# Attention and max-of-three feed-forward on one core: scaled float16 pairs with resident weights, exponentials in place in PSUM, weighted sums as one column-tiled step

## The chip, the cores and the metric

The kernel runs on one core of one Trainium2 chip. The metric is device time in microseconds (us). Before the change the median of three runs is 1806.76 us (1802.73 to 1811.37).

## What is computed

Eight batches, twelve heads, 448 tokens, 64 numbers per head. Queries and keys are divided by their root mean square over the 64 numbers and multiplied by a gain each; softmax attention follows; the heads of a batch are put side by side to a 3584x768 matrix x, and a feed-forward layer takes the elementwise maximum of three products:

```
q_n, k_n = rmsnorm(q, g_q), rmsnorm(k, g_k)
scores = q_n @ k_n.T / sqrt(64);  attn = softmax(scores)
x = (attn @ v), heads side by side                  # 3584 x 768
h = max(x @ w1, x @ w2, x @ w3)                      # 3584 x 768
out = h @ w_out
```

The four weights come as float64, everything else and the output are float32: the kernel reads a weight as pairs of 32-bit words and puts the float32 together with bit operations ("decode").

## The kernel before, in words

**Groups.** The work is cut into 48 groups g (six pairs of heads in each of eight batches). Per group the two heads' queries and keys are loaded in rows (load_q, load_kv, L167 to L193), squared and summed (squares L196, inv_rms L207, its power on POOL at L218), scaled (scale_q L221, scale_k L239), split into two float16 parts, high and low (part_rows L256), and turned to columns by a DMA transpose (turn_rows L267). A product of two numbers in two parts takes three matmuls (TERMS L317: high by high, high by low, low by high).

**Softmax.** The 448 queries of a group are four chunks c of 112. scores (L319) writes a chunk into a PSUM tile sc of two banks, one per head; the pool ps_s has two such tiles. scores is called for chunks 0 and 1 together and later for 2 and 3 together. softmax (L338) takes the row maximum on DVE (L340), a product (nm, L342) and two exponentials on ACT (L348) that write a float32 tile p in SBUF; after them sc is free. weights (L355) takes the reciprocal of the sums (rs, L359 and L362), the scaled high part on ACT (L365) and the low part on DVE (L366), which reads p and the high part pp from SBUF. turn_weights (L372) turns pp with a DMA transpose issued by SP (L377).

**Weighted sums.** add_values (L383) is called once per step with one block u of keys: the stationary operand is a block of v in both parts, 128 columns wide (64 high, 64 low), the moving one a part of the weights; the high and low columns come out in two halves of the partitions, in one PSUM tile per head (av, pool ps_a of two). fold (L403) adds the halves with one ACT and one DVE instruction per head (L409, L410), and finish (L415) splits x into a high part on ACT and a low part on POOL (L418, L419), both in fp32r (a float32 form that TensorE takes in one pass). The scale of v is found per group by a matmul with ones into a corner of sc (bound_v L288, L290) and three small DVE instructions, L292 to L297; PE and SP have their order written by hand, and the scores of the second two chunks stand behind that corner.

**Feed-forward.** ffn (L515) is a generator. layer1 (L449) does, per block ft of 128 outputs and per j of the three weights, 18 matmuls of 448 columns (L458) in six pieces of three; layer2 (L494) does per 128 tokens and half of the outputs 18 matmuls of 384 columns (L502). Before a layer1 unit, fetch (L428) loads its 384 KB of float32 weights from a scratch array in DRAM, and split_w (L437) makes high and low parts: an ACT cast (L112) and a POOL subtraction (L113). This is done anew for every batch, 144 times. The units' results are maxed on DVE (L472) and split on ACT and POOL (L477, L478).

**Decode.** prep_w (L147) loads 768 KB of float64 words, works on them with five DVE instructions (L124 twice, L129, L133, L137) and has SP store the float32 weights to the scratch (L156). prep_wo (L159) keeps w_out on chip. DECODES (L33) says how many of the 24 blocks are done in each of the first nine groups.

**Order.** The loop at L592 has eight steps i per group. In each, three times, one piece of feed-forward is put into PE's queue (ffn_third L537), so 24 pieces, 72 matmuls, per group; a fourth where two batches wait. The feed-forward of batch b enters the queue at g = 6(b+1)+1, i = 1. The order on PE and SP is the program's (manual schedule, L545); on DVE, ACT and POOL the framework's scheduler sets it. SP issues every DMA, one after the other, and stands still at a DMA whose data isn't ready.

Of the kernel before, what the change touches and what calls it, by code (L numbers as in the profile page):

```python
# [8 lines left out]
F32R = mybir.dt.float32r  # L9
# [8 lines left out]
P = 128  # L18
# [5 lines left out]

QK_UP = 2.0 ** 10
V_UP = 2.0 ** 14
P_UP = 2.0 ** 15

LEAST = 1e-30
# [3 lines left out]
DECODES = (2, 2, 2, 2, 3, 2, 4, 4, 3)  # L33
# [3 lines left out]
def qknorm_attention_maxout_ffn_kernel(  # L37
# [45 lines left out]
    LEFT = S - 3 * P  # L83

    const = ctx.enter_context(tc.tile_pool(name="const", bufs=1))
    sb = ctx.enter_context(tc.tile_pool(name="sb", bufs=2))
    dram = ctx.enter_context(tc.tile_pool(name="dram", bufs=1, space=bass.MemoryType.DRAM))
    ps_s = ctx.enter_context(tc.tile_pool(name="ps_s", bufs=2, space=bass.MemoryType.PSUM))
    ps_a = ctx.enter_context(tc.tile_pool(name="ps_a", bufs=2, space=bass.MemoryType.PSUM))
    ps_m = ctx.enter_context(tc.tile_pool(name="ps_m", bufs=2, space=bass.MemoryType.PSUM))  # L90


    warm = const.tile([P, 1], F32, name="warm")
# [4 lines left out]
    HALVES = (slice(0, 64), slice(64, 128))  # L98
    ones = const.tile([P, P], F32, name="ones")
    nc.vector.memset(ones, 1.0)  # L100
# [6 lines left out]

    wo_sb = const.tile([P, NFT, 2, DO], F32R, name="wo_sb")
    w_scr = {}

    def split(dst_hi, dst_lo, src):
        nc.scalar.copy(dst_hi, src)  # L112
        nc.gpsimd.tensor_tensor(out=dst_lo, in0=src, in1=dst_hi.bitcast(F32), op=ALU.subtract)  # L113

    def decode(raw):
# [6 lines left out]
        for dt, least in ((I16, TINY - 0x8000), (U16, TINY)):  # L122
            top = raw.bitcast(dt).rearrange("p (n t) -> p n t", t=4)[:, :, 3]
            nc.vector.tensor_scalar(  # L124
                out=top, in0=top, scalar1=float(least), scalar2=None, op0=ALU.max
            )
        f = sb.tile([P, 2, S], F32R, name="d_f", tag="xt", bufs=12)
        f = f.rearrange("p a b -> p (a b)")[:, :DM].bitcast(U32)
# [12 lines left out]
        return f.bitcast(F32)  # L141

    def raw_tile():
        t = sb.tile([P, 2, 2, S], F32R, name="raw", tag="ht", bufs=3)
        return t.rearrange("p a t s -> p (a t s)")[:, :2 * DM].bitcast(U32)

    def prep_w(ft, j):  # L147
        w = (w1, w2, w3)[j].bitcast(U32)
        raw = raw_tile()
        nc.sync.dma_start(  # L150
            out=raw.rearrange("p (c f) -> p c f", c=NCT),
            in_=w[:, 2 * ft * P:2 * (ft + 1) * P].rearrange("(c p) f -> p c f", p=P),
        )
        f = decode(raw)
        scr = dram.tile([P, NCT * P], F32, name=f"wscr_{ft}_{j}")
        nc.sync.dma_start(out=scr, in_=f)  # L156
        w_scr[ft, j] = scr

    def prep_wo(ft):  # L159
        raw = raw_tile()  # L160
        nc.sync.dma_start(out=raw, in_=w_out.bitcast(U32)[ft * P:(ft + 1) * P, :])
        split(wo_sb[:, ft, 0, :], wo_sb[:, ft, 1, :], decode(raw))
# [14 lines left out]
    def load_kv(g, name, src):  # L177
        b, pr = divmod(g, NP)
        t = sb.tile([P, 8, D], F32, name=name, bufs=2)
        rows = src[b, 2 * pr:2 * pr + 2]  # L180
        nc.sync.dma_start(
            out=t.rearrange("p (h c) d -> p h c d", h=2)[:, :, 0:3],
            in_=rows[:, 0:3 * P].rearrange("h (p c) d -> p h c d", c=3),
        )
        for h in range(2):
            nc.sync.dma_start(out=t[HALVES[h], 3], in_=rows[h, 3 * P:S])  # L186
        st.setdefault(g, {})[name] = t[:, 0:7]

    def load_k(g):
        load_kv(g, "kr", k)  # L190

    def load_v(g):
        load_kv(g, "vr", v)  # L193
# [62 lines left out]
    def part_rows(g, what):  # L256
# [3 lines left out]
        parts = sb.tile([rows, 2, 4 * P], F16, name=what + "p", bufs=2)  # L260
# [17 lines left out]


    def largest_v(g):  # L280
        s = st[g]
        s["most"] = sb.tile([P, 1], F32, name="most", bufs=2)
        nc.vector.tensor_reduce(  # L283
            s["most"], s["vr"].rearrange("p n d -> p (n d)"), axis=AX, op=ALU.max,
            apply_absolute_value=True,
        )

    def bound_v(g, corner):  # L288
        s = st[g]
        nc.tensor.matmul(corner, ones, s.pop("most"), start=True, stop=True)  # L290
        scales = sb.tile([P, 3], F32, name="vscale", bufs=3)
        nc.vector.tensor_scalar(  # L292
            out=scales[:, 0:1], in0=corner, scalar1=LEAST, scalar2=1.0 / V_UP,
            op0=ALU.max, op1=ALU.mult,
        )
        nc.vector.reciprocal(scales[:, 1:2], scales[:, 0:1])
        nc.vector.tensor_scalar(  # L297
            out=scales[:, 2:3], in0=scales[:, 0:1], scalar1=1.0 / P_UP, scalar2=None,
            op0=ALU.mult,
        )  # L300
        s["v_scales"] = scales


    def prep_v(g):
        s = st[g]
        vr, scales = s.pop("vr"), s.pop("v_scales")
        vp = sb.tile([P, 7, 2, D], F16, name="vp", bufs=2)
        nc.scalar.activation(vp[:, :, 0], vr, AF.Copy, scale=scales[:, 1:2])
        nc.vector.scalar_tensor_tensor(
            out=vp[:, :, 1], in0=vr, scalar=scales[:, 1:2], in1=vp[:, :, 0],  # L310
            op0=ALU.mult, op1=ALU.subtract,
        )
        s["vp"], s["v_down"] = vp, scales[:, 2:3]
# [3 lines left out]
    TERMS = ((0, 0), (0, 1), (1, 0))  # L317

    def scores(g, chunks, bound=None):  # L319
        s = st[g]  # L320
        qt, kt = s["qs"], s["ks"].rearrange("p a c r -> p a (c r)")
        for c in chunks:
            sc = ps_s.tile([P, 2, 512], F32, name="sc", tag="s")
            s["sc", c] = sc
        if bound is not None:
            bound_v(bound, s["sc", chunks[0]][:, 0, S:S + 1])
        for c in chunks:
            sc = s["sc", c]
            for n, (qp, kp) in enumerate(TERMS):
                for h, rows in enumerate(HALVES):  # L330
                    nc.tensor.matmul(  # L331
                        sc[:QP, h, :S], qt[rows, qp, c], kt[rows, kp, KEYS[h]],
                        start=n == 0, stop=n == len(TERMS) - 1,
                    )


    def softmax(g, c):
        sc = st[g].pop(("sc", c))  # L338
# [6 lines left out]
        p = sb.tile([QP, 2, S], F32, name="p", bufs=3)  # L345
        sm = sc[:QP, 1, S + 8:S + 10]
# [5 lines left out]
        st[g]["p", c] = p, sm  # L352


    def weights(g, c):  # L355
        s = st[g]
        p, sm = s.pop(("p", c))
        rs = sb.tile([QP, 2], F32, name="rs", bufs=3)
        nc.vector.tensor_scalar(  # L359
            out=rs, in0=sm, scalar1=SUM_EPS, scalar2=1.0 / P_UP, op0=ALU.add, op1=ALU.mult  # L360
# [3 lines left out]
        for h in range(2):  # L364
            nc.scalar.activation(pp[:, 0, h], p[:, h], AF.Copy, scale=rs[:, h:h + 1])  # L365
            nc.vector.scalar_tensor_tensor(  # L366
                out=pp[:, 1, h], in0=p[:, h], scalar=rs[:, h:h + 1], in1=pp[:, 0, h],
                op0=ALU.mult, op1=ALU.subtract,
            )
# [13 lines left out]
    def add_values(g, u):  # L383
# [314 lines left out]
```

## Time and profile before

| | |
|---|---|
| profiled execution | 1815.75 us, its span 1814.0 us |
| granted TensorE clock, mean | 0.819 |
| busy, share of the span | PE 65%, DVE 61%, POOL 55%, ACT 48% |
| DMA | 228.59 MB, mean 126 GB/s |
| DMA queue's busy share of 16 engines | 55.4% |

PE is TensorE (matmuls), PEld its weight loads, DVE VectorE, ACT ScalarE, POOL GpSimd, SP the queue that issues DMAs. A row of a group view has line, engine, operation, tiles out<-in, shape and count, then busy time and the mean ns of one, then the engine's idle time just before these instructions and who ended it. Scores of a group are 24 matmuls of L331, so the n-th group begins at its first one. By them the first group begins 24 us into the span, the eighth (where the first feed-forward starts) at 331 us, the tenth (after the last decode) at 435 us, the last one at 1661 us.

### The profile page before, as it was taken

What the parts mean: (1) busy time and instruction counts of PE and PEld (TensorE: products, weight loads), DVE (VectorE), ACT (ScalarE), POOL (GpSimd) and SP (SyncE); (2) the same over time, 40 slices, a digit from 0 to 9 for tenths busy, and PEclk for the clock granted to TensorE, in tenths of its full rate; (3) what the DMA queues carried; (4) which work ended last, traced back from release to release, by engine and by line L of the source; (5) the groups of instructions that cost most, each with busy time, mean ns of one, the idle gap of its engine ahead of it and who ended that gap; (6) DMA issues with size and microseconds to landing.
All of it is one profiled execution on the core that took longest, in us unless ns stands there. A gap on an engine that the chain in (4) does not pass through costs nothing.

```text
span 1814.0 us, 18436 instructions
## 1 busy us (share of the span) xinstructions
PE 1187.3 (65%) x5616; PEld 906.5 (50%) x5616; DVE 1112.6 (61%) x1905; ACT 866.7 (48%) x1760; POOL 1000.2 (55%) x862
## 2 busy tenths in 40 slices
PE   1222312346777886866668777978776767868898
PEld 0111101234656565754546555756664646656798
DVE  4667565598656667575666666666676666666110
ACT  3433333234556655554545555656655554555331
POOL 6333132277765776475655666577856565543261
PEclk9955555677879888987888888888897877888999
DMA  2654545556657475655456556667664655665331
GB/s 79 145 134 114 144 109 142 124 145 140 147 124 160 114 153 115 132 123 128 106 113 142 133 117 128 137 139 168 145 130 117 125 124 102 140 128 120 96 106 52
DMA packets 498595, 228.59 MB, mean 126 GB/s; under 512 B 424256, under 2 KB 473408, under 8 KB 498496
## 3 DMA queue, kind: packets, MB, share of 16 engines
q1 hardware_dynamic: 498496, 227.42, 55.4%
q8 instruction: 44, 0.72, 0.2%
q14 instruction: 55, 0.45, 0.1%
HBM read 108.59 MB, written 18.09 MB: 70 GB/s over the span
## 4 chain that ended last, share of the span: by engine, by line
DVE 28%; DMA 20%; PE 13%; SPq 10%; issue 10%; ACT 9%; POOL 9%; ACTq 0%; POOLq 0%; DVEq 0%
DVE pp L366 12%; PE acc L458 7%; DMA wf<-wscr 7%; DMA raw<-in_moe_w_dram 4%; PE acc L502 4%; DVE raw L124 3%; ACT p L348 3%; DVE sc L340 3%; ACT pp L365 3%; SPq L377 3%; POOL wt L113 3%; DMA vr<-in_v_dram 3%; DMA kr<-in_k_dram 2%; SPq L186 2%; SPq L170 2%
## 5 line engine op out<-in xcount | busy, mean ns | idle before, releaser
L458 PE MATMUL acc<-xt,wt 128*128 128x448 f32 x2592 | 705.4, 419 | 215.0 <-POOL wt L113 101.7
L458 PEld LDWEIGHTS acc<-xt,wt 128*128 128x128 f32 x2592 | 542.2, 212 | 330.9 <-POOL wt L113 128.7
L366 DVE SCALAR_TENSOR_TENSOR pp<-p,rs,pp 112x448 f16<-112x448 f32 x384 | 426.5, 1147 | 75.0 <-ACT pp L365 74.6
L331 PE MATMUL sc<-kt,qt 64*112 64x448 f16 x1152 | 174.0, 444 | 281.4 <-DMA qt<-qp 214.8
L113 POOL TENSOR_TENSOR wt<-wf,wt 128x768 fp32r<-128x768 f32 x144 | 266.3, 1850 | 159.5 <-ACT wt L112 131.1
L348 ACT ACTIVATE p<-sc,nm,down 112x448 f32<-112x448 f32 x384 | 269.6, 731 | 170.2 <-DVE nm L342 158.5
L331 PEld LDWEIGHTS <-qt 64*112 64x112 f16 x1152 | 105.6, 158 | 322.6 <-DMA qt<-qp 222.6
L365 ACT ACTIVATE pp<-p,rs 112x448 f16<-112x448 f32 x384 | 232.0, 671 | 72.6 <-DVE rs L362 66.9
L218 POOL TENSOR_TENSOR ri<-ss,half_neg 128x7 f32<-128x7 f32 x96 | 159.8, 1665 | 177.8 <-DVE ss L213 139.7
L397 PE MATMUL av<-pt,vp 128*128 128x448 f16 x576 | 185.3, 417 | 76.2 <-DVE nm L342 23.4
L340 DVE TENSOR_REDUCE sc<-sc 112x2 f32<-112x896 f32 x192 | 206.2, 1092 | 37.2 <-PE sc L331 35.5
L112 ACT CAST wt<-wf 128x768 fp32r<-128x768 f32 x144 | 120.7, 838 | 208.4 <-DMA wf<-wscr 180.3
L502 PE MATMUL acc<-wo_sb,ht 128*128 128x384 f32 x864 | 190.0, 371 | 31.3 <-ACT ht L477 16.1
L502 PEld LDWEIGHTS acc<-wo_sb,ht 128*128 128x128 f32 x864 | 164.3, 203 | 45.9 <-POOL ht L478 17.8
L397 PEld LDWEIGHTS <-vp 128*128 128x128 f16 x576 | 40.1, 109 | 159.8 <-issue 145.4
L204 POOL TENSOR_TENSOR sq<-qr 112x512 f32<-112x512 f32 x40 | 43.0, 1075 | 138.9 <-DMA qr<-in_q_dram 138.8
L204 POOL TENSOR_TENSOR sq<-kr 128x448 f32<-128x448 f32 x40 | 38.3, 958 | 142.7 <-DMA kr<-in_k_dram 132.0
L212 DVE TENSOR_REDUCE ss<-sq 128x7 f32<-128x448 f32 x96 | 62.0, 646 | 85.5 <-POOL sq L204 71.3
L472 DVE TENSOR_TENSOR m<-acc,m 128x448 f32<-128x448 f32 x96 | 59.1, 616 | 86.6 <-PE acc L458 86.1
L410 DVE SCALAR_TENSOR_TENSOR x<-av,vscale,x 64x448 f32<-64x448 f32 x96 | 65.3, 680 | 64.7 <-ACT x L409 63.2
L283 DVE TENSOR_REDUCE most<-vr 128x1 f32<-128x448 f32 x48 | 29.7, 618 | 122.1 <-DMA vr<-in_v_dram 122.1
L124 DVE TENSOR_SCALAR raw<-raw 128x768 int16<-128x768 int16 (+1 forms) x48 | 66.1, 1377 | 52.0 <-DMA raw<-in_moe_w_dram 48.0
(56 smaller groups left out, 1267.0 us busy)
## 6 DMA issues: line engine op xcount, KB each, us to landing
wf<-wscr SPq DMA_DIRECT2D x144, 384.0 KB, 3.8
raw<-in_moe_w_dram SPq DMA_DIRECT2D x18, 768.0 KB, 5.4
qr<-in_q_dram SPq DMA_DIRECT2D x48, 224.0 KB, 3.8
kr<-in_k_dram SPq DMA_DIRECT2D x48, 192.0 KB, 3.4
vr<-in_v_dram SPq DMA_DIRECT2D x48, 192.0 KB, 3.2
wscr<-d_f SPq DMA_DIRECT2D x18, 384.0 KB, 2.6
raw<-in_moe_w_out_dram SPq DMA_DIRECT2D x6, 768.0 KB, 5.4
pt<-pp SPq DMA_TRANSPOSE x192, 3.9
```

Source lines behind the costliest of these rows:

```text
L112: nc.scalar.copy(dst_hi, src)
L113: nc.gpsimd.tensor_tensor(out=dst_lo, in0=src, in1=dst_hi.bitcast(F32), op=ALU.subtract)
L124: nc.vector.tensor_scalar(out=top, in0=top, scalar1=float(least), scalar2=None, op0=ALU.max)
L218: nc.gpsimd.tensor_tensor(out=ri, in0=ss, in1=half_neg[:rows, :n], op=ALU.pow)
L331: nc.tensor.matmul(sc[:QP, h, :S], qt[rows, qp, c], kt[rows, kp, KEYS[h]], start=n == 0, stop=n == len(TERMS) - 1,)
L340: nc.vector.tensor_reduce(low, sc[:QP, :, :S], axis=AX, op=ALU.max, negate=True)
L348: nc.scalar.activation(p[:, h], sc[:QP, h, :S], AF.Exp, bias=nm[:, h:h + 1], scale=down[:QP], accum_out=sm[:, h:h + 1],)
L365: nc.scalar.activation(pp[:, 0, h], p[:, h], AF.Copy, scale=rs[:, h:h + 1])
L366: nc.vector.scalar_tensor_tensor(out=pp[:, 1, h], in0=p[:, h], scalar=rs[:, h:h + 1], in1=pp[:, 0, h], op0=ALU.mult, op1=ALU.subtract,)
L397: nc.tensor.matmul(s["av"][u // 4][:, :S], vp[:, u], pt[:, 7 * part + u], start=u % 4 == 0 and part == 0, stop=False,)
L458: nc.tensor.matmul(acc[:, :S], wt[:, wp, c], xs[c][:, xp], start=(c == 0 and n == 0), stop=(c == NCT - 1 and n == 2),)
L502: nc.tensor.matmul(acc[:, :HW], lhs, wo_sb[:, f, wp, half * HW:(half + 1) * HW], start=(f == 0 and n == 0), stop=(f == NFT - 1 and n == 2),)
```

## The change

- **Weights.** Each decoded block is scaled by its largest number and split into a float16 pair, kept in SBUF for the whole run (w_sb for w1 to w3, wo_sb for w_out). The DRAM scratch, fetch and split_w go. xt, ht and hx become float16 pairs too. All low parts of these splits, xt's and ht's included, are now a DVE scalar_tensor_tensor; POOL does none of them. The largest number of a block is found with a DVE maximum over each row, a matmul with the identity (largest) and, one step later, a matmul with ones (spread), both in PE's queue. The scales come out again as per-partition factors in the instructions that empty PSUM after layer1 and layer2. In decode the two int16 maxima move from DVE to POOL.
- **Exponentials.** They are written over the scores in PSUM; weights reads them from there, so that a tile sc stays taken until the low part is made. Chunks come singly, at i = 0, 2, 4, 6, and weights of a chunk at the step after.
- **Weighted sums.** A group's matmuls come together at i = 4 of the next group: three terms, v's columns 64 wide, the two heads in the two column halves of the array and of one PSUM tile. fold goes; finish reads av from PSUM.
- **Order.** turn_weights stands one step after weights, stores one step after their copy. v is loaded six groups ahead (seven groups of v in group 0), its scale taken per batch. DECODES becomes 3, 3, 3, 3 and then six times 2, and w_out's parts are made when the last block is scaled. The feed-forward of batch b enters at g = 6(b+1), i = 5. Loads of k and v are split by head (four DMAs each for three).

The diff, cut to its core:

```diff
-DECODES = (2, 2, 2, 2, 3, 2, 4, 4, 3)
+DECODES = (3, 3, 3, 3, 2, 2, 2, 2, 2, 2)
...
+    def later(slots, work):
+        due.setdefault(clock[0] + slots, []).append(work)
...
+    def largest(column, done):
+        nc.tensor.matmul(marks[0:1, 0:P], column, ident, start=True, stop=True)
+        top = sb.tile([1, 1], F32, name="top", bufs=2)
+        nc.vector.tensor_reduce(top, marks[0:1, 0:P], axis=AX, op=ALU.max)
+        def spread():
+            at = n_marks[0]
+            n_marks[0] += 1
+            nc.tensor.matmul(marks[:, at:at + 1], ones, top, start=True, stop=True)
+            done(marks[:, at:at + 1])
+        later(1, spread)
...
+    w_sb = const.tile([P, NFT * NJ, 2, NCT * P], F16, name="w_sb")
+    wo_sb = const.tile([P, NFT + 1, 2, DO], F16, name="wo_sb")
...
-            nc.vector.tensor_scalar(
+            nc.gpsimd.tensor_scalar(
                 out=top, in0=top, scalar1=float(least), scalar2=None, op0=ALU.max
...
+    def split(hi, lo, src, by):
+        nc.scalar.activation(hi, src, AF.Copy, scale=by)
+        nc.vector.scalar_tensor_tensor(
+            out=lo, in0=src, scalar=by, in1=hi, op0=ALU.mult, op1=ALU.subtract
+        )
...
+    def prep_block(n):
...
+        decode(raws[n], f)
+        later(2, load_raw)
+        most = sb.tile([P, 1], F32, name="w_row", bufs=2)
+        row_largest(most, f)
...
+                split(w_sb[:, n, 0], w_sb[:, n, 1], f, up)
...
+        later(1, lambda: largest(most, scale))
...
     def softmax(g, c):
...
-        p = sb.tile([QP, 2, S], F32, name="p", bufs=3)
         for h in range(2):
             nc.scalar.activation(
-                p[:, h], sc[:QP, h, :S], AF.Exp, bias=nm[:, h:h + 1], scale=down[:QP],
-                accum_out=sm[:, h:h + 1],
+                sc[:QP, h, :S], sc[:QP, h, :S], AF.Exp, bias=nm[:, h:h + 1],
+                scale=down[:QP], accum_out=sc[:QP, 1, S + 8 + h:S + 9 + h],
             )
...
+            split(pp[:, 0, h], pp[:, 1, h], sc[:QP, h, :S], rs[:, h:h + 1])
...
+    def add_values(g):
+        s = st[g]
+        vp, pt = s["vp"], s["pt"]
+        av = ps_a.tile([P, 512], F32, name="av", tag="a")
+        for u in range(4):
+            for n, (wp, vpart) in enumerate(TERMS):
+                for h, half in enumerate(HALVES):
+                    rows = half if u == 3 else slice(0, P)
+                    group = 3 if u == 3 else 4 * h + u
                     nc.tensor.matmul(
+                        av[half, :S], vp[rows, group, vpart], pt[rows, 7 * wp + group],
+                        start=u == 0 and n == 0, stop=u == 3 and n == len(TERMS) - 1,
                     )
...
+        split(xt[:, 0], xt[:, 1], av[:, :S], 1.0 / P_UP)
...
+        nc.vector.scalar_tensor_tensor(
+            out=m, in0=acc[:, :S], scalar=top, in1=m, op0=ALU.mult, op1=ALU.max
+        )
...
+            split(ht[:, 0], ht[:, 1], m, h_down[:, ft:ft + 1])
...
+            tick()
+            if g < G and i % 2 == 0:
+                scores(g, i // 2)
                 softmax(g, i // 2)
+            if w >= 0 and i == 4:
+                add_values(w)
+                finish(w, x_of[w // NP])
...
+            if g < G and i % 2 == 1:
+                weights(g, i // 2)
+                later(1, lambda g=g, c=i // 2: turn_weights(g, c))
```

More of the change, by code (lines that the diff above doesn't have):

```diff
@@ L159, in prep_wo @@
[L159 to L162, printed above, removed]
+    def split(hi, lo, src, by):
+        nc.scalar.activation(hi, src, AF.Copy, scale=by)
+        nc.vector.scalar_tensor_tensor(
+            out=lo, in0=src, scalar=by, in1=hi, op0=ALU.mult, op1=ALU.subtract
+        )
+    blocks = [("in", ft, j) for ft in range(NFT) for j in range(NJ)]
+    blocks += [("out", ft, 3) for ft in range(NFT)]
@@ L259, in part_rows @@
         rows = n.shape[0]
-        parts = sb.tile([rows, 2, 4 * P], F16, name=what + "p", bufs=2)
+        parts = sb.tile([rows, 2, 4 * P], F16, name=what + "p", bufs=1)
         nc.scalar.copy(parts[:, 0], n)
@@ L276, in turn_rows @@
         s[what + "s"] = t
+    v_rows = {}
+    v_down = const.tile([P, B], F32, name="v_down")
+    v_up = const.tile([P, B], F32, name="v_up")
     def largest_v(g):
[L281 to L301, printed above, removed]
+        b, pr = divmod(g, NP)
+        if pr == 0:
+            v_rows[b] = sb.tile([P, NP], F32, name="v_rows", bufs=2)
+        row_largest(v_rows[b][:, pr:pr + 1], st[g]["vr"].rearrange("p n d -> p (n d)"))
@@ L658, in qknorm_attention_maxout_ffn_kernel @@
                     turn_rows(g + 1, "q")
[L659 to L665 removed]
+    while queue or due:
+        tick()
+        for _ in range(3):
+            ffn_third()
 _INS = ['q', 'k', 'v', 'g_q', 'g_k', 'moe_w1', 'moe_w2', 'moe_w3', 'moe_w_out']
```

372 lines of the change are left out of this document (176 added, 196 removed).

## The prediction

> **What bounds the kernel now.** First I cut the span into its stages with the view of busy time in windows: the first seven groups, attention and decode alone (25 to 331 us); three groups with decode and feed-forward; the 38 groups of the steady stage (435 to 1661); the last group; the end. Columns: length, busy time (instructions) of PE, PEld, DVE, ACT and POOL, granted clock, DMA share, GB/s.
>
> ```profile
> core 0: us, PE busy (x) PEld busy (x) DVE busy (x) ACT busy (x) POOL busy (x), PEclk, DMA share, GB/s
> 25.00:331.00 306.00, 68.81 (x280) 30.98 (x280) 189.80 (x328) 107.15 (x223) 102.09 (x92) 0.64 0.52 128
> 331.00:435.00 104.00, 53.19 (x215) 36.88 (x217) 86.17 (x110) 38.94 (x75) 57.56 (x40) 0.73 0.65 157
> 435.00:1661.00 1226.00, 924.82 (x4397) 710.91 (x4395) 803.99 (x1401) 666.39 (x1368) 767.74 (x664) 0.85 0.60 129
> 1691.00:1814.00 123.00, 114.87 (x598) 107.60 (x596) 9.49 (x15) 29.63 (x48) 44.08 (x33) 0.98 0.26 80
> ```
>
> In the steady stage a group takes 1226/38 = 32.3 us. PE is busy 24.3 of them, DVE 21.2, POOL 20.2, ACT 17.5: no engine is full, though PE is nearest. At the end PE is busy 115 of 123 us at nearly full clock. So each stage has its own limit. The groups of the steady stage, by line:
>
> ```profile
> L458 PE MATMUL acc<-xt,wt 128*128 128x448 f32 x2043 | 577.0, 427 | 181.9 <-POOL wt L113 81.2 <-ACT wt L112 66.4 <-DVE nm L342 19.6
> ...
> L366 DVE SCALAR_TENSOR_TENSOR pp<-p,rs,pp 112x448 f16<-112x448 f32 x304 | 366.9, 1246 | 60.6 <-ACT pp L365 60.3
> ...
> L340 DVE TENSOR_REDUCE sc<-sc 112x2 f32<-112x896 f32 x152 | 162.6, 1091 | 5.1 <-PE sc L331 3.5
> ...
> L331 PE MATMUL sc<-kt,qt 64*112 64x448 f16 x912 | 126.6, 418 | 49.3 <-DVE vscale L292 36.5 <-DMA qt<-qp 10.5 <-DVE rs L359 2.2
> ...
> L112 ACT CAST wt<-wf 128x768 fp32r<-128x768 f32 x113 | 94.7, 838 | 155.4 <-DMA wf<-wscr 149.8 <-PE acc L458 4.3 <-PE sc L331 0.6
> ...
> L410 DVE SCALAR_TENSOR_TENSOR x<-av,vscale,x 64x448 f32<-64x448 f32 x76 | 51.8, 681 | 43.3 <-ACT x L409 42.1
> ...
> L409 ACT ACTIVATE x<-av,vscale 64x448 f32<-64x448 f32 x76 | 47.8, 629 | 35.9 <-PE av L392 34.3
> ```
>
> L458's first row says why PE stands still: it waits for POOL's and ACT's parts of the weights. The waits of that stage, PE's and then SP's:
>
> ```profile
> PE acc L458 <- POOL wt L113: 81.2, 51, 4.0
> PE acc L458 <- ACT wt L112: 66.4, 26, 5.4
> PE sc L331 <- DVE vscale L292: 36.5, 38, 3.9
> ...
> SPq L377 <- DVE pp L366: 451.5, 73, 16.0
> ```
>
> PE is idle (1226 - 924.8)/38 = 7.9 us per group; 147.6/38 = 3.9 of these wait for the weight parts and 36.5/38 = 1.0 for the scale of v. SP stands at the transposes of the weights (L377) for want of DVE's low parts, with the loads of k, q and v behind it in the same queue.
>
> How fast is PE when nothing hinders it? Two rows of the chain at the end, and the PE timeline of a warm stretch (start us, length us):
>
> ```profile
> 1726.55 57.47 PE acc L458 x286
> 1784.02 25.01 PE acc L502 x144
> ```
>
> ```profile
> 1661.30 1.47 PE L331 MATMUL sc<-kt,qt 64*112 64x448 f16 x12
> ...
> 1670.81 0.28 PE L290 MATMUL sc<-most,ones 128*128 128x1 f32 x2
> ...
> 1674.02 0.55 PE L397 MATMUL av<-pt,vp 128*128 128x448 f16 x2
> 1674.25 2.14 PE L458 MATMUL acc<-xt,wt 128*128 128x448 f32 x9
> 1676.22 0.55 PE L397 MATMUL av<-pt,vp 128*128 128x448 f16 x2
> ```
>
> 286 matmuls of 448 columns in 57.47 us are 201 ns each in fp32r, 144 of 384 columns 174 ns. From 1674.02 to 1676.22 lie two float16 matmuls and nine in fp32r: 2.20 - 9 x 0.201 = 0.39 us for the two, 195 ns each. **Float16 buys PE nothing per matmul.** Twelve score matmuls take 1.47 us, since two run side by side.
>
> A group's feed-forward is 54 x 0.201 + 21 x 0.174 = 14.5 us (54 is 2043/38; 21 is layer2's 36 matmuls for each of 3.5 blocks of tokens, over six groups). Scores add 2.9, weighted sums 14 x 0.2 = 2.8, the corner of v 2 x 0.28: 20.8 at full clock, against 24.3 measured. Half clock costs 3.5 us a group.
>
> **The change, part by part.** *Weights resident.* Per group 3 loads of 384 KB, 3 ACT casts and 3 POOL subtractions go, with PE's 3.9 us of waiting. POOL loses L113 and the two subtractions of xt and ht:
>
> ```profile
> L113 POOL TENSOR_TENSOR wt<-wf,wt 128x768 fp32r<-128x768 f32 x114 | 210.7, 1848 | 112.4 <-ACT wt L112 102.4 <-issue 4.5 <-DMA wf<-wscr 3.6
> ...
> L478 POOL TENSOR_TENSOR ht<-m,ht 128x448 fp32r<-128x448 f32 x38 | 50.0, 1317 | 11.3 <-ACT ht L477 11.0
> ...
> L419 POOL TENSOR_TENSOR xt<-x,xt 128x448 fp32r<-128x448 f32 x38 | 43.3, 1140 | 29.4 <-ACT xt L418 29.4
> ```
>
> (210.7 + 50.0 + 43.3)/38 = 8.0, so 12.2 of 20.2 us stay. ACT loses (94.7 + 47.8)/38 = 3.8 with L112 and L409: 13.7 of 17.5.
>
> *Low parts on DVE, read from PSUM.* L366 has two inputs in SBUF, and its row over the whole run shows that something holds it:
>
> ```profile
> L366 DVE SCALAR_TENSOR_TENSOR pp<-p,rs,pp x384: 646/685/5594, 35.4 to 1686.2; 112x448 f16<-112x448 f32 x192
> ...
> L366 DVE SCALAR_TENSOR_TENSOR pp<-p,rs,pp 112x448 f16<-112x448 f32 x56 | 38.0, 702 | 12.6 <-ACT pp L365 12.6
> ```
>
> Mostly it takes 0.685 us, at worst 5.6, and in the steady stage 366.9/304 = 1.21 of DVE's time. In the first seven groups, the second of these rows, it is 0.702; POOL is busy 33% there against 63%. L410, with one input in PSUM, has mean 0.681. Now the first input of all eight lies in PSUM: I take 0.68, saving 8 x 0.53 = 4.2 us; the bound on the other side is no saving. fold goes (51.8/38 = 1.4), xt's and ht's low parts come (2 x 0.68, up to 2 x 1.21): DVE 21.2 - 4.2 - 1.4 + 1.5 = 17.1 us, or 22 without any saving. Both are below PE's pace, so this part has cover; without it a busier DVE would set the group at 22 or more.
>
> *Exponentials in PSUM.* No row shows ACT writing PSUM. From the SBUF version at 0.7 us, a third less or more is 2 us of ACT time per group, on 13.7: hidden. The price is elsewhere, in how long sc is taken (a rival).
>
> *Weighted sums.* 24 matmuls of 64 columns in two column halves: as 12 pairs, if they overlap as the scores' row halves do, 12 x 0.2 + 0.25 to start = 2.65; one after the other 5.05. I take the pairs, the scores being the nearest row. The Trainium skill, "TensorEngine Tiling (Array Packing)", speaks against it in "Key Properties", where a change of tiling mode drains the array, and in "Restrictions and Gotchas", where column tiling shuts off the fast weight load. No run so far shows column tiles. By that rule the sum would lie nearer the second figure.
>
> *Queues.* SP loses three loads of weights a group. It gains one issue each for k and v; turn_weights moves one step back, past the next step's first wait for pp, so SP's 451.5 us of standing shrink, as pp is a step old; the q, k and v loads behind profit. v, six groups early, is not late. AV at i = 4 waits on PE for the transpose issued at i = 0 of that step, four steps of feed-forward before: covered if SP is not late; otherwise FFN pieces queue behind it. Scores no longer wait for the corner of v.
>
> *Steady group.* PE: 14.5 + 4 x 0.74 + 2.65 = 20.1 at full clock. Idle: 7.9 - 3.9 - 1.0 = 3.0, which I let stand for the new waits, since the old ones behind it (nm, ht, pt) remain in kind. Half clock follows idling: 3.5 x 3.0/7.9 = 1.3. Together 24.4 us, 7.9 less than now.
>
> *Early groups.* What decode costs, and what the SP queue does there:
>
> ```profile
> L124 DVE TENSOR_SCALAR raw<-raw 128x768 int16<-128x768 int16 (+1 forms) x32 | 41.0, 1282 | 41.4 <-DMA raw<-in_moe_w_dram 41.2
> ...
> L331 PE MATMUL sc<-kt,qt 64*112 64x448 f16 x170 | 36.4, 573 | 222.0 <-DMA qt<-qp 204.3 <-DVE rs L359 14.1 <-DVE vscale L292 3.6
> ...
> L137 DVE SCALAR_TENSOR_TENSOR d_f<-raw,d_f 128x768 uint32<-128x768 uint32 x16 | 18.2, 1139 | 0.2
> ...
> L133 DVE SCALAR_TENSOR_TENSOR d_f<-raw,d_f 128x768 uint32<-128x768 uint32 x16 | 16.9, 1055 | 0.2
> ...
> L129 DVE TENSOR_SCALAR d_f<-raw 128x768 uint32<-128x768 uint32 x16 | 12.6, 790 | 0.3
> ```
>
> ```profile
> SPq L156 <- DVE d_f L137: 103.7, 9, 12.2
> ```
>
> 170 score matmuls, 24 a group, are seven groups in 306 us, 43.7 each, DVE busy only 62%. The scores wait 204 us for the q transposes, and these stand in SP's queue behind the store to the scratch (L156), which waits for decode's last step. That store goes. What is late next is DVE. Its attention work is (189.8 - 16 blocks x (2 x 1.28 + 0.79 + 1.06 + 1.14))/7 = 14.4, less 0.7 for fold against xt: 13.7. A block costs 0.79 + 1.06 + 1.14 = 3.0 and the new row maximum (768 numbers; 896 take 1.09), 0.95, the split 768/448 x 0.68 = 1.17, and small ones, 0.4: 5.5. Three blocks make 30.2 us a group, two 24.7. No row shows DVE as the bound; its shares are 62% here and 66% later, PE's at the end 93%. I take 85%: 4 x 35.5 + 2.6 x 29.1 + 4 for the seven loads of v in group 0 = 222 us, 286 at 66%, 203 at 93%. Before it 26 us to the first scores, one for the identity. PE's two waits per block (largest, spread) lie one step after their DVE work; PE idles there anyway.
>
> Feed-forward starts at group 6, i = 5. From there to group 10 two blocks of w_out per group: DVE 17.1 + 2 x 4.35 + six splits over 3.4 groups (2.1) = 27.9, at 85% 32.8, times 3.4 = 111 us. Then 38.6 steady groups up to i = 5 of the last, 38.6 x 24.4 = 942. Then the last batch alone: 324 x 0.201 + 144 x 0.174 = 90, with 7 for the last x, copy and store: 97.
>
> **Sum:** 26 + 222 + 111 + 942 + 97 = 1398 for the span, against 1814; 1400 with the 1.75 that the profiled execution has around it. It was 1815.75 where the median is 1806.76, a factor of 0.995: **1393 us**.
>
> **The rivals.** *Full clock throughout.* The granted clock is 0.98 at the end where PE has no long gaps, 0.85 where it has. If the gaps that remain are short, the 1.3 us go: 38.6 x 1.3 = 50 less, 1343; if the idle time of 3 goes by half too, 1285. Against: that nm, ht and pt still make gaps. The Trainium skill, "TensorE: Matmul & The Clock Gate", Part 1, has the gate fall to half only after an idle window of about 3.4 us, which speaks for this case; the trace agrees in that the early stage, with its long waits, shows 0.64.
>
> *The score tiles stay taken.* There are two, and now each is held until the low part. How long are two chunks in flight today, from their first matmul to their last low part? Two cases, a slow and a quick one:
>
> ```profile
> 1073.35 2.49 PE L331 MATMUL sc<-kt,qt 64*112 64x448 f16 x12 [0.71 <-DVE vscale L292]
> ...
> 1091.39 1.27 DVE L366 SCALAR_TENSOR_TENSOR pp<-p,rs,pp 112x448 f16<-112x448 f32 x2
> ```
>
> ```profile
> 1672.74 1.34 PE L331 MATMUL sc<-kt,qt 64*112 64x448 f16 x12 [1.65 <-DVE vscale L292]
> ...
> 1684.52 2.40 DVE L366 SCALAR_TENSOR_TENSOR pp<-p,rs,pp 112x448 f16<-112x448 f32 x2 [0.58 <-ACT pp L365]
> ```
>
> 1092.66 - 1073.35 = 19.3 and 1686.92 - 1672.74 = 14.2 us. If two chunks still take 14.2, a group takes 28.4, and the time is 1393 + 38.6 x 4.0 = 1547. For it: the chain is long. Against: single chunks a step apart don't wait for each other's halves, DVE's 1.21 becomes 0.68 and POOL releases it; the bare chain of a chunk (0.74 + 1.09 + two exponentials, two splits and four small steps) is near 7.
>
> *Slower: the same, at 19.3.* Then PE stands behind the scores at 38.6 us a group: 1393 + 38.6 x 14.2 = 1941. It decides from 35.1 us a group, two chunks in 17.5 us. The row above has this, but with DVE held for 4.55 us by POOL's work, of which 40% goes.
>
> *Column halves don't overlap.* 2.4 us more of PE per group: 1393 + 93 = 1486. That step of the change then does not do what it says.
>
> **How the numbers follow.** The forecast has 0.52, the full clock 0.21, the tiles at 14.2 us 0.15, the columns 0.07, slower 0.04, and 0.01 a mixture near no change. About 0.5% is what a measurement can tell here. Faster 0.95, same 0.01, slower 0.04. The range reaches from the full clock with half the idle time and DVE at 93% (1285 - 19, about 1270) to the tiles at 14.2 us (1550); the early stage at 66% (1457) lies inside it.
>
> **What would show it.** Steady groups of 24.4 us with PE busy above 85%, granted clock above 0.9, and matmuls of 201 and 174 ns as before; no wait of L458 for weight parts; the low part of pp near 0.68 us with a small spread; first feed-forward near 250 us; POOL at 12 us a group. I am wrong if scores wait for sc to be freed (PE idle behind a DVE low part), if DVE is fuller than PE in the steady stage, or if AV's matmuls stand 0.2 us apart singly.

## The result, and the profile after

The changed kernel takes 1405.25 us (1404.18 to 1407.23), against 1805.52 for the kernel before in the same comparison: a ratio of 0.778, 95% interval 0.776 to 0.780. The profiled execution has a span of 1402.4 us and a mean granted clock of 0.915. Its busy time in windows, cut as before: start, attention and decode, decode with feed-forward, the steady groups (37 of them, from group 10 to group 47), and the end.

```profile
core 0: us, PE busy (x) PEld busy (x) DVE busy (x) ACT busy (x) POOL busy (x), PEclk, DMA share, GB/s
0.00:32.00 32.00, 0.00 (x0) 0.00 (x0) 11.07 (x21) 5.65 (x9) 23.80 (x30) 1.00 0.25 70
32.00:238.00 206.00, 66.78 (x334) 31.01 (x335) 169.16 (x346) 93.81 (x189) 178.78 (x100) 0.72 0.61 148
238.00:360.00 122.00, 88.75 (x467) 40.77 (x468) 103.38 (x205) 60.14 (x127) 106.04 (x71) 0.82 0.65 138
360.00:1271.00 911.00, 755.75 (x4529) 369.84 (x4528) 606.68 (x1293) 538.34 (x1156) 415.15 (x458) 0.96 0.61 121
1271.00:1402.00 131.00, 122.49 (x709) 65.60 (x708) 29.40 (x53) 31.17 (x59) 2.37 (x8) 1.00 0.16 39
```

A steady group takes 911/37 = 24.6 us, PE is busy 20.4 of them, DVE 16.4, ACT 14.6, POOL 11.2, and the granted clock is 0.96. The groups of that stage by line, and PE's longest waits in it:

```profile
L498 PE MATMUL acc<-xt,w_sb 128*128 128x448 f16 x1971 | 414.7, 367 | 2.9 <-DVE m L509 2.9
...
L187 DVE SCALAR_TENSOR_TENSOR pp<-sc,rs,pp 112x448 f16<-112x448 f32 x296 | 200.5, 679 | 88.7 <-ACT pp L186 88.1
...
L186 ACT ACTIVATE pp<-sc,rs 112x448 f16<-112x448 f32 x296 | 186.4, 636 | 179.5 <-DVE pp L187 111.5 <-issue 26.9 <-ACT sc L437 25.3
...
L420 PE MATMUL sc<-kt,qt 64*112 64x448 f16 x890 | 120.5, 373 | 139.6 <-DVE pp L187 139.3
```

```profile
PE sc L420 <- DVE pp L187: 139.3, 78, 4.5
PE marks L141 <- DVE top L136: 10.0, 5, 4.3
PE acc L498 <- DVE m L509: 2.9, 2, 1.6
PE acc L549 <- DVE ht L187: 1.9, 3, 1.0
```

POOL's and ACT's weight parts are gone from PE's waits, and one row has nearly all that is left: in 139.3 of the 155 us in which PE is idle it waits for a low part (L187), so that the next chunk's scores (L420) get a tile. ACT has a new wait of the same kind: its high part of the second head (L186) waits 112 us for DVE's low part of the first. Both only read the tile, and before, when p lay in SBUF, the one did not wait for the other.

The low parts themselves, over the whole run, as the view of one line has them (ns min/median/max):

```profile
L187 DVE SCALAR_TENSOR_TENSOR pp<-sc,rs,pp x384: 660/677/686, 42.4 to 1296.3; 112x448 f16<-112x448 f32 x192
```

Before, the spread went from 646 to 5594 ns; with the first input in PSUM it is 26 ns. The end, in the chain of waits, and one group's weighted sums in PE's timeline:

```profile
1296.99 3.30 DMA pt<-pp
...
1300.42 2.58 PE av L478 x24
1303.00 9.86 PE acc L549 x60
1312.86 61.29 PE acc L498 x324
1374.15 23.41 PE acc L549 x144
```

```profile
849.23 0.78 PE L420 MATMUL sc<-kt,qt 64*112 64x448 f16 x6
849.93 2.58 PE L478 MATMUL av<-pt,vp 128*64 128x448 f16 x24
852.45 3.10 PE L549 MATMUL acc<-wo_sb,ht 128*128 128x384 f16 x18
```

24 matmuls in two column halves take 2.58 us, so they run in pairs. 324 matmuls of 448 columns take 61.29 us, 189 ns each (201 before), 144 of 384 columns 163 (174 before).

### The profile page after: what moved, and what is told of

The parts are those of the page before. It is cut to its first block, busy times and chain, and to the rows that moved or that the text cites. A ratio compares the mean times of both kernels' runs of the same rounds, so it can differ in the third digit from the quotient of the medians.

```text
span 1402.4 us, 18577 instructions
## 1 busy us (share of the span) xinstructions
PE 1033.8 (74%) x6032; PEld 507.2 (36%) x6032; DVE 919.7 (66%) x1916; ACT 729.1 (52%) x1538; POOL 726.1 (52%) x666
## 5 line engine op out<-in xcount | busy, mean ns | idle before, releaser
L498 PE MATMUL acc<-xt,w_sb 128*128 128x448 f16 x2592 | 542.8, 366 | 2.9 <-DVE m L509 2.9
L186 ACT ACTIVATE pp<-sc,rs 112x448 f16<-112x448 f32 x384 | 241.5, 635 | 248.5 <-DVE pp L187 155.6
L498 PEld LDWEIGHTS <-w_sb 128*128 128x128 f16 x2592 | 250.6, 101 | 280.9 <-issue 82.3
L437 ACT ACTIVATE sc<-sc,nm,down 112x448 f32<-112x448 f32 x384 | 268.1, 698 | 153.0 <-DVE nm L433 94.0
L420 PE MATMUL sc<-kt,qt 64*112 64x448 f16 x1152 | 170.2, 401 | 231.7 <-DVE pp L187 198.6
L187 DVE SCALAR_TENSOR_TENSOR pp<-sc,rs,pp 112x448 f16<-112x448 f32 x384 | 259.5, 679 | 102.6 <-ACT pp L186 101.9
L420 PEld LDWEIGHTS <-qt 64*112 64x112 f16 x1152 | 83.8, 136 | 296.8 <-issue 256.6
L168 POOL TENSOR_SCALAR raw<-raw 128x768 int16<-128x768 int16 (+1 forms) x48 | 163.9, 3414 | 32.2 <-DMA raw<-in_moe_w_dram 18.3
L549 PE MATMUL acc<-wo_sb,ht 128*128 128x384 f16 x864 | 154.9, 334 | 3.0 <-DVE ht L187 2.1
L478 PE MATMUL av<-pt,vp 128*64 128x448 f16 (+1 forms) x1152 | 134.8, 378 | 3.8 <-DMA pt<-pp 2.1
L549 PEld LDWEIGHTS <-ht 128*128 128x128 f16 x864 | 82.2, 100 | 73.6 <-issue 19.9
L509 DVE SCALAR_TENSOR_TENSOR m<-acc,w_top,m 128x448 f32<-128x448 f32 x96 | 65.0, 677 | 66.3 <-PE acc L498 66.2
L134 PE MATMUL marks<-ident,w_row 128*1 128x128 f32 x48 | 12.0, 343 | 98.3 <-DVE w_row L147 91.1
```

Of the source, the lines that this page charges most:

```text
L168: nc.gpsimd.tensor_scalar(out=top, in0=top, scalar1=float(least), scalar2=None, op0=ALU.max)
L186: nc.scalar.activation(hi, src, AF.Copy, scale=by)
L187: nc.vector.scalar_tensor_tensor(out=lo, in0=src, scalar=by, in1=hi, op0=ALU.mult, op1=ALU.subtract)
L420: nc.tensor.matmul(sc[:QP, h, :S], qt[rows, qp, c], kt[rows, kp, KEYS[h]], start=n == 0, stop=n == len(TERMS) - 1,)
L437: nc.scalar.activation(sc[:QP, h, :S], sc[:QP, h, :S], AF.Exp, bias=nm[:, h:h + 1], scale=down[:QP], accum_out=sc[:QP, 1, S + 8 + h:S + 9 ...
L478: nc.tensor.matmul(av[half, :S], vp[rows, group, vpart], pt[rows, 7 * wp + group], start=u == 0 and n == 0, stop=u == 3 and n == len(TERMS ...
```

## The experiments

Theory A: two score tiles, each held from its first score matmul to its last low part, set the steady group. Worked out from the trace as the mean over chunks 40 to 189 of (end of the last low part - start of the first score matmul), a tile is held 11.3 us; with 1.0 us until its next chunk, two tiles give 2 x 12.3 = 24.6 us a group of four chunks. That this sum gives the group is so by construction, since each tile takes every second chunk. What speaks for theory A is that the 1.0 us is so short and that PE waits for it; the runs test whether it is the cause. Theory B: PE's work sets it, as the forecast had it, and the waits fill time that would be idle anyway. Times are medians, beside 1405.25.

**One tile instead of two**

```diff
-    ps_s = ctx.enter_context(tc.tile_pool(name="ps_s", bufs=2, space=bass.MemoryType.PSUM))
+    ps_s = ctx.enter_context(tc.tile_pool(name="ps_s", bufs=1, space=bass.MemoryType.PSUM))
```

> The changed kernel with one score tile instead of two, nothing else changed: the suspected wait is doubled. Theory A: a chunk begins only when the one before it has its last low part; a tile is held 8 to 9 us where nothing else is in flight, so a group takes 4 x 9 = 36 us and the whole about 1405 + 38.6 x 12 = 1870 us, near or above the kernel before. Theory B: feed-forward matmuls fill most of the wait; under 1550 us.

1983.08 us, slower than the kernel before by 10% (ratio 1.101, 1.098 to 1.104). The waits of the whole run:

```profile
PE sc L420 <- DVE pp L187: 737.4, 172, 13.0
```

A group takes 36.6 us. A tile is held 9.1 us here and taken again 0.1 us later. Theory A gave 36 a group; theory B, under 1550 us, is out. The whole is 113 us more than theory A's 1870: group 10 begins at 489 us instead of 360, and that price had left the early groups as they were.

**A tile for each head**

```diff
-        sc = ps_s.tile([P, 2, 512], F32, name="sc", tag="s")
+        sc = [ps_s.tile([P, 512], F32, name=f"sc{h}", tag=f"s{h}") for h in range(2)]
...
-        nc.vector.tensor_reduce(low, sc[:QP, :, :S], axis=AX, op=ALU.max, negate=True)
+        for h in range(2):
+            nc.vector.tensor_reduce(
+                nm[:, h:h + 1], sc[h][:QP, :S], axis=AX, op=ALU.max, negate=True
+            )
```

> The changed kernel with a score tile of its own for each head (two tiles of one bank per chunk, as many banks as before; row maxima per head, sums in SBUF). In the changed kernel's trace PE waits 143 us of the 939 us steady stage for a low part to free a score tile, a chunk's tile is taken 11.3 us in the mean from its first matmul to its last low part, and ACT's second high part waits 118 us for DVE's first low part. Theory A, the score tiles set the steady group (two in flight, group = 2 x (11.3 + about 1) = 24.6 us): the second high part no longer waits for the first low part, each bank comes free by itself, a tile is held about 1 us less, a group is about 2 us shorter, and the time 1300 to 1350 us. Theory B, PE's work sets it and the waits only fill what would be idle anyway: within 10 us of 1405.

1372.3 us (ratio 0.7625, 0.760 to 0.765), 33 less: the way of theory A, and less than it had priced. A chunk is held 10.7 us to its last low part, ACT no longer waits for DVE's low parts, and a group takes 23.6 us. That is 1.0 us less, where theory A had 2; and of these 37 x 1.0 us, 15 are lost ahead of them, since group 10 begins that much later. PE's waits in its steady stage (374 to 1247 us):

```profile
PE sc L420 <- DVE pp L187: 81.7, 88, 4.0
PE marks L141 <- DVE top L136: 9.6, 5, 3.3
```

**Exponentials to SBUF**

```diff
+        p = sb.tile([QP, 2, S], F32, name="p", bufs=3)
...
-                sc[:QP, h, :S], sc[:QP, h, :S], AF.Exp, bias=nm[:, h:h + 1],
+                p[:, h], sc[:QP, h, :S], AF.Exp, bias=nm[:, h:h + 1],
...
-            split(pp[:, 0, h], pp[:, 1, h], sc[:QP, h, :S], rs[:, h:h + 1])
+            split(pp[:, 0, h], pp[:, 1, h], p[:, h], rs[:, h:h + 1])
```

> The changed kernel with the exponentials written to a tile in SBUF again (three of them; one buffer fewer of v and two fewer of x make the room), so that a score tile is free after them and the low part has both inputs in SBUF. Theory A: PE's 143 us of waiting for the low part go and the tile is held about 6 us instead of 11; low parts take 0.85 to 1.2 us instead of 0.68, which costs DVE 1.5 to 4 us of a group that then has room; 1330 to 1400 us. Rival C, that reading from PSUM was what made the low part cheap and this outweighs the tiles: slower than the changed kernel, 1440 to 1500 us, with low parts of 1.1 us and more.

1328.81 us (ratio 0.737, 0.734 to 0.740): 76 us less than with the exponentials in place, just below theory A's range. Rival C is out. The group row of the low part, and PE's longest waits in the steady groups (360 to 1203 us):

```profile
L187 DVE SCALAR_TENSOR_TENSOR pp<-p,rs,pp 112x448 f16<-112x448 f32 x384 | 301.9, 809 | 77.2 <-ACT pp L186 76.2 <-DMA vr<-in_v_dram 0.7
```

```profile
PE av L480 <- DMA pt<-pp: 23.5, 17, 2.5
PE sc L420 <- DVE rs L449: 22.0, 21, 2.5
PE acc L500 <- DVE m L511: 11.2, 12, 2.5
```

PE's wait for a score tile falls from 139 to 22 us. These 22 are the second row: the sums of the exponentials still lie in the tile, and L449 reads them. (So it is in the kernel before, where L359 reads the sums: there too a tile sc is free only after that read, not already after the exponentials.) The low part is dearer, 809 ns over the whole run against 1147 in the kernel before, and 784 against 1246 in the steady groups. PE is busy 745 of 843 us, and a group takes 22.8, 1.8 less; PE's idle time falls by less than its wait for tiles, from 4.2 to 2.6 us a group, as other waits grow.

**The same part alone, in the kernel before**

```diff
-        p = sb.tile([QP, 2, S], F32, name="p", bufs=3)
...
-                p[:, h], sc[:QP, h, :S], AF.Exp, bias=nm[:, h:h + 1], scale=down[:QP],
+                sc[:QP, h, :S], sc[:QP, h, :S], AF.Exp, bias=nm[:, h:h + 1], scale=down[:QP],
...
-        st[g]["p", c] = p, sm
+        st[g]["p", c] = sc, sm
```

> The kernel before, with the exponentials left in PSUM and the low parts read from there: this part of the change alone. Theory A, the score tiles: a pair of chunks is now held until its last low part, 14 to 19 us in the kernel before less about 2 for the cheaper low parts, two pairs a group with about 2 us between: 28 to 38 us a group instead of 32.3, and the time 1700 to 1950 us, no gain to speak of. Rival C, the cheap low part from PSUM (0.68 instead of 1.25 us) is what counts: DVE loses 4.2 us a group, and the time is under 1680 us.

1692.02 us, ratio 0.940 (0.937 to 0.942) to the kernel before: a gain of 108 us, a little under theory A's span and near to rival C's. So the same edit gains 108 us there and costs 76 us here. The low part's row, and PE's waits for a low part to free a tile:

```profile
L365 DVE SCALAR_TENSOR_TENSOR pp<-sc,rs,pp 112x448 f16<-112x448 f32 x384 | 252.4, 679 | 106.7 <-ACT pp L364 103.4
```

```profile
PE sc L290 <- DVE pp L365: 78.6, 24, 10.0
...
PE sc L331 <- DVE pp L365: 20.8, 19, 3.4
```

In the kernel before the low part falls from 1147 to 679 ns, and the chain from the first score to the last low part gets shorter with it, 12.4 us instead of 15.3. Still a tile is held longer than before, when L359's read freed it after 10.2 us, and that costs there too: 99 us of PE's waiting in these two rows (L290 writes into the corner of sc, and so waits for the tile as L331 does). The cheaper low part is worth more. In the changed kernel the low part from SBUF takes only 809, so there is little to win against the longer hold of the tile.

What makes the low part dear can be read from the traces by sorting all 384 by whether a POOL instruction runs beside them. In the kernel before, the 102 alone take 676 ns in the mean and the 282 beside POOL 1318; in this run, with one input in PSUM, the 78 alone take 678 and the 306 beside POOL 679. So POOL's work lengthens the form with two inputs in SBUF and not the other.

Why 809 and not 1147? Worked out from the traces as the sum over all low parts of (time - 676 ns): 181 us in the kernel before, 51 with exponentials to SBUF in the changed one. By what POOL ran beside them, 68 of the 181 lie beside the subtraction of the weight parts (L113), which is gone; 87 lie beside the scaling and splitting of q and k, which is there in both kernels, but coincides less with the low parts in the second. That the chunks come singly would explain it; no run tested that.

**Weights not streamed, in the kernel before**

```diff
-        wt = parts[unit]
+        wt = parts[unit % 2]
...
-                split_w(unit + 1)
+                split_w(min(unit + 1, 1))
...
-                fetch(unit + 2)
+                fetch(min(unit + 2, 1))
```

> The kernel before, with the weights of the first two feed-forward units loaded and split once and used for all 144 units (it leaves the other units' loads and splits out, so its output isn't the reference's). It shows what streaming and splitting the weights anew costs the kernel before. The prediction's step: PE's 3.9 us of waiting per steady group go, with about half as much of half clock behind it, and POOL's 5.5 us that held DVE's low parts: 5 to 6 us in each of some 38 groups and some in the last batch, 1570 to 1630 us. If the wait is only exchanged for another (scores behind the corner of v, low parts on DVE): over 1700 us.

1576.08 us, ratio 0.875 (0.873 to 0.878): 224 us less. A group takes 26.8 us instead of 32.3, 5.5 less, within what the prediction's step gives. Its group rows, and its steady stage from group 9 on in the view of windows:

```profile
L458 PE MATMUL acc<-xt,wt 128*128 128x448 f32 x2592 | 631.1, 393 | 8.2 <-ACT m L469 6.6 <-DVE m L472 1.6
...
L366 DVE SCALAR_TENSOR_TENSOR pp<-p,rs,pp 112x448 f16<-112x448 f32 x384 | 375.1, 1022 | 48.5 <-ACT pp L365 48.2
```

```profile
411.00:1428.00 1017.00, 830.11 (x4391) 666.95 (x4387) 738.42 (x1411) 583.16 (x1261) 578.65 (x551) 0.92 0.56 112
```

PE waits 8 us for its units in the whole run, where the page of the kernel before has 215, and without L113 the low part falls to 1022 ns. Of the 5.5 us, 3.0 are idle time of PE (7.9 a group before, (1017 - 830.1)/38 = 4.9 now: the wait for the weight parts was 3.9, and the waits for v's scale and for the transposes grew), and 2.5 are busy time, with the granted clock at 0.92 instead of 0.85.

**Float16 for the second product alone, in the kernel before**

```diff
-    wo_sb = const.tile([P, NFT, 2, DO], F32R, name="wo_sb")
+    wo_sb = const.tile([P, NFT, 2, DO], F16, name="wo_sb")
...
-                keep["ht"] = sb.tile([P, 2, 2, S], F32R, name="ht", tag="ht", bufs=3)
+                keep["ht"] = sb.tile([P, 2, 2, S], F16, name="ht", bufs=3)
```

> The kernel before, with the second product alone (h and w_out) in float16 pairs, unscaled, everything else as it was: what the number format does to the rate of a matmul. If it is the format, the 144 matmuls of 384 columns at the end take 163 ns each, as in the changed kernel, instead of 174; if it is something else of the change, 174. The 448-column matmuls in fp32r stay at 201 ns either way.

The last rows of its chain of waits:

```profile
1723.17 59.06 PE acc L462 x286
1782.23 23.43 PE acc L506 x144
```

For this product it is the format: 144 matmuls in 23.43 us are 163 ns each, and their weight loads take 104 ns instead of 203. The 286 matmuls in fp32r take 206 ns in the mean because the granted clock was 0.97 in that stretch (1723 to 1782 us), which costs some 1.7 us; without that they take 201. No run changed the format of the 448-column product alone. The program ran once, so nothing is said of its time (1812.35 us).

**Decode's maxima on DVE**

```diff
-            nc.gpsimd.tensor_scalar(
+            nc.vector.tensor_scalar(
```

> The changed kernel with decode's two int16 maxima on DVE again instead of POOL. In the first seven groups of the changed kernel POOL is busy 201 of 229 us, with 3.4 us for each of these maxima, and DVE 187 of 229. If POOL is what bounds that stage: POOL loses 6.8 us per block, DVE gains 2.1, and the whole is 15 to 40 us shorter than 1405. If DVE bounds it, as the prediction said: DVE gains 24 x 2.1 = 50 us of work, the whole is 20 to 50 us longer.

1401.9 us, ratio 0.778 (0.776 to 0.781): no difference. Start and first groups of this kernel in windows:

```profile
core 0: us, PE busy (x) PEld busy (x) DVE busy (x) ACT busy (x) POOL busy (x), PEclk, DMA share, GB/s
0.00:26.00 26.00, 0.00 (x0) 0.00 (x0) 12.37 (x23) 5.43 (x9) 17.65 (x27) 1.00 0.31 86
26.00:230.00 204.00, 69.75 (x332) 33.20 (x333) 183.36 (x379) 94.47 (x190) 83.58 (x73) 0.77 0.59 150
```

POOL falls from 179 of 206 to 84 of 204 us, DVE goes from 82% to 90%, and the groups take as long. The first scores come 6 us earlier, which is gone again by group 10 (360.3 against 359.7 us). Neither of the two expectations came true: POOL at 87% wasn't the bound, and DVE had room for 14 us more.

**The largest number's matmul one step later** (on top of exponentials to SBUF)

```diff
-        later(1, lambda: largest(most, scale))
+        later(2, lambda: largest(most, scale))
```

> The changed kernel with exponentials to SBUF (as in the third run above, 1329 us), and the matmul that finds a block's largest number one step later in PE's queue. In the first seven groups PE stands 128 us at these matmuls for DVE's row maximum, with the scores queued behind. If that delays the early groups: 10 to 30 us less than 1329. If DVE and POOL, both over 80% busy there, set them: within 5 us.

1311.02 us, ratio 0.728 (0.726 to 0.730), 18 less. Here is PE's wait for the row maximum (L134), over the whole run without and then with this edit:

```profile
PE marks L134 <- DVE w_row L147: 128.0, 20, 14.7
```

```profile
PE marks L134 <- DVE w_row L147: 74.0, 12, 10.6
```

It falls from 128 to 74 us, and group 10 begins at 344.5 instead of 360.2 us. So the stop was not free: in PE's order the next chunk's scores stand behind it.

**The weighted sums two steps earlier (i = 2 instead of 4)**

```diff
-            if w >= 0 and i == 4:
+            if w >= 0 and i == (4 if g == 1 else 2):
...
-            if w >= 0 and i == 2 and g > 1:
+            if w >= 0 and i == 1 and g > 1:
                 prep_v(w)
```

> The changed kernel with the weighted sums of a group at i = 2 of the next group instead of i = 4 (v's parts one step earlier, so that they are there): the half step of the change undone. In the changed kernel PE hardly waits for the transposed weights (2 us in the whole run), and a transpose takes 3.4 us from issue to landing after about 1.5 us of issue. If the half step hides that: the last chunk's low part ends about when the scores of i = 2 may start, PE stands some 4 us a group behind it, and the whole takes 100 to 190 us longer, 1505 to 1595 us. If the waits for score tiles already give the time: within 25 us of 1405.

1464.99 us, ratio 0.814 (0.811 to 0.816): 60 us more, between the two expectations. PE's waits from 360 to 1330 us:

```profile
PE av L478 <- DMA pt<-pp: 74.4, 26, 4.6
PE sc L420 <- DVE pp L187: 71.7, 49, 3.9
PE av L478 <- issue: 27.6, 11, 2.7
```

The transposes are waited for, 102 us with what follows, and the score tiles give half of their 139 back: a wait in one place lets another run out.

**Together**

```diff
-            if len(queue) > 1:
+            if len(queue) > 1 or i == 3:
                 ffn_third()
...
-        decode(raws[n], f)
+        decode(raws[n], f, nc.vector if n == 0 else nc.gpsimd)
```

> What the runs so far point to, together: the changed kernel with exponentials to SBUF and the largest number's matmul one step later (1311 us), and two small ones: the first block's int16 maxima on DVE (the first scores came 6 us earlier when all of them were there) and one more piece of feed-forward per group at i = 3, so that the second product of the last batch but one is not left over for the end (60 matmuls, 10 us, in the changed kernel). If all of it adds up: 1290 to 1303 us; if PE has no room in the steady groups for the added piece: 1303 to 1312 us.

1308.97 us, ratio 0.7266 (0.724 to 0.729), not told apart from 0.7283 without the two small edits, and in the range given for PE having no room. Its end:

```profile
1213.51 2.58 PE av L480 x24
1216.09 1.57 PE acc L551 x9
1217.66 61.29 PE acc L500 x324
1278.94 23.41 PE acc L551 x144
```

The leftover of the second product at the end falls from 60 matmuls to 9, but the steady groups take 23.0 us instead of 22.6: its time was moved, not saved. Still, this and the run before it beat both kernels, by 94 to 96 us the changed one.

## Why the prediction was right, and where it was not

**The terms of the sum.** First scores: 26 us forecast, 32.4 measured. To the first feed-forward matmul: 222, and 255.7 - 32.4 = 223. To group 10: 111, and 359.7 - 255.7 = 104. To the last weighted sums: 942, and 1300.4 - 359.7 = 941. The end: 97, and 1402.4 - 1300.4 = 102. The start is longer by what POOL does ahead of the first rows: with decode's maxima on DVE it is 26 us. The end has 60 matmuls, 9.86 us, of the last batch but one in it, against which the faster matmuls stand.

**The steady group: right in size, wrong in make-up.** The forecast was 20.1 of work, 1.3 of half clock and 3.0 idle. Measured: work 53.3 x 0.189 + 20.4 x 0.163 + 4 x 0.74 + 2.58 = 18.9 (1971 and 756 matmuls in 37 groups), 20.4 - 18.9 = 1.5 of busy time beyond it, most of it half clock, and idle (911 - 755.75)/37 = 4.2. The step "float16 buys PE nothing per matmul" failed: it rested on two matmuls between fp32r ones, and a run of float16 alone goes at 189 and 163 ns, which the run with the second product in float16 puts down to the format for the 163. The step that let 3.0 us of idle time stand "since the old ones behind it (nm, ht, pt) remain in kind" failed too: these waits came to 0.1 us, and 3.8 of the 4.2 are the wait for a score tile. The two errors cancel, 1.2 us less work against 1.2 us more idle time, so that 24.4 against a measured 24.6 is luck. By its own sign ("I am wrong if scores wait for sc to be freed") the prediction is wrong in this step. With the exponentials in SBUF idle time is 2.6 us a group, near the 3.0, and the old kinds of waits are back.

**Weights resident.** Right in size: 5.5 us a group in the kernel before, where the prediction had 3.9 of waiting and, by its own rule, 3.5 x 3.9/7.9 = 1.7 of half clock. The parts are 3.0 of idle time and 2.5 of busy time, as other waits took some of the 3.9. In the kernel before it is worth 224 us, beside the 400 of the whole change.

**Low parts from PSUM.** The price was right (0.68 taken, 0.679 measured). What it is worth was not seen: from SBUF it costs 0.81 in the changed kernel, where the kernel before has 1.15, so that 0.13 us on each of eight instructions is all that the longer hold of the tiles buys.

**The rivals.** That the score tiles stay taken, which had a chance of 0.15, was the mechanism at work: with a tile for each head, and with tiles freed earlier, the wait shrinks and the kernel gets faster. Its size was off: two chunks take 12.3 us (11.3 held, 1.0 between), not 14.2. The slower rival is this with 17.5 us or more for two chunks; the run with one tile, at 18.3, shows that such a kernel is indeed slower than before. Column halves overlap. The full clock nearly came, 0.96; what it lacks, 0.04 x 24.6 = 1.0 us a group, is near the 1.3 forecast. The rule that the prediction cites from the Trainium skill ("TensorE: Matmul & The Clock Gate", Part 1), that the clock falls only after an idle window of 3.4 us, is not borne out as the prediction used it: in the steady groups the clock fell to half 19 times, and near 14 of these PE had no wait as long as 3.4 us. A window that was busy for less than some 0.42 was enough (last section). The rule of the Trainium skill, "TensorEngine Tiling (Array Packing)", that a change of tiling mode drains the array does not decide here: the whole of a group's sums, the changes of mode with it, is 2.58 us where twelve pairs alone, at 0.189, would be 2.27.

**Early groups.** Right by 1 us, with DVE at 82% where 85% was taken. The 85% was chosen between 66% and 93% and no row gave it, so a hit this close is luck: DVE had room for 14 us more of work, and PE's stops at largest, which the prediction held to be free ("PE idles there anyway"), cost something: 18 us where exponentials go to SBUF. What bounds those groups is not settled beyond that: neither DVE's nor POOL's load alone.

## What to carry to other kernels

A PSUM tile that is kept for a second reader is a buffer held longer: count tiles in flight and time the hold before counting the copies saved, and see who else is made to wait when two engines read one tile. The same edit may pay in one kernel and cost in the next, as its gain (here a VectorE instruction that GpSimd's work no longer lengthens) depends on what else runs beside it. A sum that comes out right is no proof of its terms; PE's waits by releaser told in four rows which rival was at work.

## What the runs showed of the hardware that was not expected

At full clock and back to back, a matmul in fp32r took 201 ns for 448 columns and 174 for 384, one in float16 189 and 163; its weight load took 0.20 to 0.21 us in fp32r and 0.10 in float16. GpSimd took 3.4 us for a maximum over 768 16-bit integers at a stride of four, for which VectorE took 1.0 at best. A VectorE instruction with two inputs in SBUF, 0.68 us where GpSimd is idle, took 1.32 us in the mean beside GpSimd's work in the kernel before and up to 5.6; with one input in PSUM it took 0.66 to 0.69 in the changed kernel, beside GpSimd or not.

The granted clock goes by windows of 3.41 us: all its changes in a trace lie on one grid of that step. Worked out from the changed kernel's trace as PE's busy share in each window: the clock fell to half after 30 windows, 29 of them busy for at most 0.42, and stayed full after 283, each busy for at least 0.42. It rose again after 29, each busy for at least 0.85. The kernel before shows the same, with 72 falls, 71 of them after at most 0.46. So a PE wait of 2 to 3 us can be enough, if it falls into one such window, to halve the clock in the next.
